# A cosformer-attention and GEGLU kernel: the first two tiles of batch 0 normalised side by side, and the turning of q tile 2 moved

## The chip, the cores and the metric

One core of one Trainium2 chip. The metric is device microseconds of one execution; lower is better. Most executions of a kernel agree within 0.3%, which here is 1 us.

## The reference

```python
def _attn_ref(q, k, v):                      # q, k, v: (8, 8, 576, 64) fp32
    ...
    def phi(x, c, s):
        r = np.maximum(x, 0.0)
        return np.concatenate([r * c, r * s], axis=-1)
    q_p = phi(q, cos_w, sin_w); k_p = phi(k, cos_w, sin_w)
    kv = np.einsum('bhsf,bhsd->bhfd', k_p, v)
    z = np.sum(k_p, axis=2)
    num = np.einsum('bhsf,bhfd->bhsd', q_p, kv)
    den = np.einsum('bhsf,bhf->bhs', q_p, z)[..., None] + 1e-06
    return num / den
# x = attention output as (4608, 512); then
# out = (gelu(x @ w_gate) * (x @ w_val)) @ w_out       with d_ff = 1536
```

The attention has no softmax. Each batch needs one 128x65 product per head ("kv", with the sum z as its 65th column), and then a numerator and a norm for each tile of 128 positions. The feed-forward part is the bulk of the work.

## The kernel before

The instruction streams are written by hand, and each engine runs its stream in program order. Block 0 of the feed-forward part needs x of batch 0, so the attention of batch 0 is a prologue that nothing can hide. The helpers and the prologue that the change touches:

```python
def numer_mm(b, t, bank, g, rows=128):           # numerators of 4 heads of tile t
    for h in range(4 * g, 4 * g + 4):
        nc.tensor.matmul(ps[0:rows, bank + g, ...], lhsT=qT[b % 2][:, t, h, 0:rows], rhs=kv[b % 2][:, h, 0:D + 1], ...)

def norm(xb, bank, g0, g1, rows=128):            # den = z-column + EPS; rec = 1/den; xb = numerator * rec
    ...
def x_by_pe(b, t, xb, bank, eng, c0=0, c1=CT):   # turn x on PE, copy to xT on eng
    ...
def q_by_pe(b, j, bank, eng, h0=0, h1=H):        # turn q tile j on PE; q_evac copies it to SBUF
    ...

# ... (cut)
kv_half(0, 0, 4, None)                           # heads 0 to 3
q_evac(0, 1, 1, "v")
dummies(2)
cast_v(0, 4, 6, "v")
cast_v(0, 6, 8, "s")
kv_evac(0, 0, 4, "v")
kv_half(0, 1, 5, "s")                            # heads 4 to 7
x0, x1 = new_xb(), new_xb()
numer_mm(0, 0, 6, 0)
norm(x0, 6, 0, 1)
dummies(1, 4)
numer_mm(0, 0, 6, 1)
sq(2, 1, "s")
norm(x0, 6, 1, 2)
sq(2, 0, "v")
numer_mm(0, 1, 0, 0)
numer_mm(0, 1, 0, 1)
norm(x1, 0, 0, 2)
x_by_pe(0, 0, x0, 4, "s", 0, 2)
dummies(2, 5)
x_by_pe(0, 0, x0, 4, "s", 2, 4)
q_by_pe(0, 2, 3, None)
# ... (cut: weight load, helpers)
gate(0, 0, 0, 128, 5)
gate(0, 1, 0, 128, 4)
X(1, 2, "s")()                                   # turn x of tile 1
q_evac(0, 2, 3, "v")
sq(3, 0, "v"), sq(3, 1, "s")
value(0, 0, 0, 128, 6)
value(0, 1, 0, 128, 7)
Y(2, 0)()                                        # numerators and norm of tile 2
gate(0, 0, 128, 128, 5)                          # "the second gate pair"
gate(0, 1, 128, 128, 4)
```

"v" is VectorE (DVE), "s" is ScalarE (ACT), PE is TensorE. To turn a tile is to transpose it by matmuls with the identity; the result is then copied from PSUM to SBUF ("evacuated") before the next matmul reads it. A gate and a value are the two products with the weights of a feed-forward unit, gelu(gate) times value is its result. The dummies are matmuls without use that keep PE busy.

## Time and profile before

| | before |
|---|---|
| time, median of 6 runs (range) | 325.81 us (325.72 to 325.93) |
| span of the profiled execution | 324.3 us |
| PE busy | 315.1 us, 97% |
| PE's share of the chain that ended last | 93% |
| kv half 1 starts (K) | 13.48 us |
| second-half x transposes of tile 0 start (X) | 16.04 us |
| second gate pair starts (C) | 18.53 us |

A busy share of 97% means that a saving counts only where PE itself waits. K, X and C are the marks that I use throughout. K follows the landing of v's heads 4 to 7 in this kernel. X starts when tile 0 is normalised. From C on the instructions of all kernels here are the same. In the timelines the columns are start, us, engine, line, operation, out<-in, shape, count, and in brackets the idle time before it and what ended that. PE's timeline of the kernel before, just ahead of C:

```profile
17.69 0.61 PE L229 MATMUL ps<-xT,wv_sb 128*128 128x128 bf16 x8
18.14 0.42 PE L170 MATMUL ps<-kv,qT 128*128 128x65 bf16 x8
18.53 0.61 PE L218 MATMUL ps<-xT,wg_sb 128*128 128x128 bf16 x8
```

Values (L229), numerators of tile 2 (L170) and gates (L218) follow each other.

### The profile page before, as it was taken

The page shows a single profiled execution, that of the slowest core. Times are in us where ns is not written, and L with a number is a line of the kernel's source. Part 1 is how long each engine was busy: PE and PEld are TensorE (multiplying, and loading weights), DVE is VectorE, ACT ScalarE, POOL GpSimd, SP SyncE. Part 2 cuts the span into 40 slices and gives each one's busy share as a digit, 9 for nine tenths or more (in the row PEclk, how much of TensorE's full clock was granted, in tenths as well). Part 3 has the DMA queues.
Part 4 walks back from the last instruction along what each step waited for, and adds up shares of the span by engine and source line. Part 5 has one row for each costly group of instructions (what it writes and reads, how often), then busy time and mean ns, then how long its engine had stood idle before and what let it go on. Part 6 is the DMA issues. An engine that isn't in the chain of part 4 may idle for free.

```text
span 324.3 us, 5829 instructions
## 1 busy us (share of the span) xinstructions
PE 315.1 (97%) x2185; PEld 167.1 (52%) x2218; DVE 168.0 (52%) x380; ACT 151.3 (47%) x271; POOL 21.7 (7%) x43
## 2 busy tenths in 40 slices
PE   7899999999999999999999999999999999999994
PEld 3587866455445544544455445544554444444443
DVE  4885776677564576366636574647454222222210
ACT  5674764853583248325642565237522222323321
POOL 2551000001100010001000100010000100100000
PEclk9999999999999999999999999999999999999999
DMA  7999999999899939991999289936333111000124
GB/s 223 287 204 275 226 307 306 324 200 172 282 222 345 219 51 194 333 236 51 195 324 242 50 153 294 301 68 124 104 73 75 32 32 34 32 32 32 37 63 98
DMA packets 88300, 55.56 MB, mean 171 GB/s; under 512 B 53072, under 2 KB 83536, under 8 KB 88272
## 3 DMA queue, kind: packets, MB, share of 16 engines
q1 hardware_dynamic: 81744, 48.84, 60.8%
q0 software_dynamic: 6096, 5.90, 10.2%
q10 hardware_dynamic: 432, 0.46, 0.4%
q8 instruction: 17, 0.28, 0.3%
q14 instruction: 11, 0.09, 0.1%
HBM read 37.75 MB, written 9.44 MB: 146 GB/s over the span
## 4 chain that ended last, share of the span: by engine, by line
PE 93%; DMA 2%; SPq 1%; DVE 1%; issue 1%; POOL 0%; ACT 0%; POOLq 0%; DVEq 0%
PE ps L218 29%; PE ps L229 29%; PE ps L259 28%; PE ps L170 3%; PE ps L154 3%; DMA vf<-in_v_dram 2%; SPq L80 1%; PE ps L277 1%; PE ps L324 1%; PE ps L343 1%; DVE vx L141 0%; ACT xT L346 0%; DVE qp L135 0%; POOL vf L98 0%; POOL qf L97 0%
## 5 line engine op out<-in xcount | busy, mean ns | idle before, releaser
L234 DVE TENSOR_TENSOR hT<-gel,ps 128x512 bf16<-128x512 f32 (+5 forms) x126 | 76.1, 607 | 89.3 <-PE ps L229 88.4
L218 PE MATMUL ps<-xT,wg_sb 128*128 128x512 bf16 (+5 forms) x492 | 111.8, 348 | 0.7
L229 PE MATMUL ps<-xT,wv_sb 128*128 128x512 bf16 (+5 forms) x496 | 111.8, 348 | 0.4
L223 ACT ACTIVATE gel<-ps 128x512 f32<-128x512 f32 (+5 forms) x126 | 67.4, 536 | 74.2 <-PE ps L218 51.9
L259 PE MATMUL ps<-wo_sb,hT 128*128 128x512 bf16 x408 | 94.3, 379 | 0.6
L218 PEld LDWEIGHTS <-wg_sb 128*128 128x128 bf16 x504 | 47.1, 98 | 44.5
L229 PEld LDWEIGHTS <-wv_sb 128*128 128x128 bf16 x504 | 45.7, 98 | 39.0
L259 PEld LDWEIGHTS <-hT 128*128 128x128 bf16 x420 | 40.8, 98 | 47.7
L288 ACT COPY o_sb<-ps 128x512 f32<-128x512 f32 x35 | 20.5, 586 | 76.2 <-PE ps L259 69.9
L185 DVE TENSOR_TENSOR xb<-ps,rec 128x512 bf16<-128x512 f32 (+2 forms) x41 | 27.8, 678 | 2.8 <-DMA xr<-xb 1.4
L182 DVE TENSOR_SCALAR den<-ps 128x8 f32<-128x8 f32 (+2 forms) x41 | 6.7, 163 | 42.2 <-PE ps L170 42.2
L137 ACT ACTIVATE kp<-kf,sin_c 128x512 bf16<-128x512 f32 (+1 forms) x41 | 25.4, 681 | 0.8 <-DMA kf<-in_k_dram 0.8
L170 PEld LDWEIGHTS <-qT 128*128 128x128 bf16 (+1 forms) x320 | 15.1, 98 | 8.3 <-issue 0.4
L137 ACT ACTIVATE qp<-qf,sin_c 128x512 bf16<-128x512 f32 x28 | 19.3, 713 | 0.1
L135 DVE TENSOR_SCALAR kp<-kf,cos_c 128x512 bf16<-128x512 f32 (+1 forms) x45 | 18.1, 450 | 1.4 <-DMA kf<-in_k_dram 1.4
L135 DVE TENSOR_SCALAR qp<-qf,cos_c 128x512 bf16<-128x512 f32 x40 | 18.2, 495 | 0.0
L209 POOL COPY xT<-xr 128x256 bf16<-128x256 bf16 x7 | 2.8, 402 | 208.7 <-DMA xr<-xb 208.7
L170 PE MATMUL ps<-kv,qT 128*128 128x65 bf16 (+1 forms) x320 | 16.6, 194 | 0.1
L154 PEld LDWEIGHTS <-kp 128*128 128x128 bf16 x320 | 10.9, 97 | 2.6 <-issue 0.7
L127 PE MATMUL ps<-hT 128*128 128x512 bf16 x33 | 10.2, 460 | 1.8 <-DVE par_i L104 1.7
L154 PE MATMUL ps<-vx,kp 128*128 128x65 bf16 x320 | 11.2, 193 | 0.1
L141 ACT CAST vx<-vf 128x1280 bf16<-128x1280 f32 (+1 forms) x9 | 9.7, 1076 | 1.2 <-DMA vf<-in_v_dram 1.2
(54 smaller groups left out, 88.6 us busy)
## 6 DMA issues: line engine op xcount, KB each, us to landing
out_dram<-o_sb SPq DMA_DIRECT2D x38, 128.0 KB, 2.4
kf<-in_k_dram SPq DMA_DIRECT2D x7, 640.0 KB, 7.3
out_dram<-o_sb SPq DMA_DIRECT2D x16, 256.0 KB, 2.9
qf<-in_q_dram SPq DMA_DIRECT2D x6, 640.0 KB, 6.2
vf<-in_v_dram SPq DMA_DIRECT2D x6, 640.0 KB, 8.7
kf<-in_k_dram SPq DMA_DIRECT2D x7, 512.0 KB, 6.2
qf<-in_q_dram SPq DMA_DIRECT2D x6, 512.0 KB, 4.9
vf<-in_v_dram SPq DMA_DIRECT2D x6, 512.0 KB, 7.8
```

The costliest lines, as they stand in the source:

```text
L127: nc.tensor.matmul(ps[:, bank, :], lhsT=junk[:, 0:128], rhs=junk, start=True, stop=True)
L135: nc.vector.tensor_scalar(d, s, col, 0.0, op0=ALU.mult, op1=ALU.max)
L137: nc.scalar.activation(d, s, AF.Relu, scale=col)
L154: nc.tensor.matmul(ps[:, bank, (h % 4) * (D + 1):(h % 4 + 1) * (D + 1)], lhsT=kp[:, j, h, :], rhs=vx[b % 2][:, j, h, 0:D + 1], start=(j == ...
L170: nc.tensor.matmul(ps[0:rows, bank + g, (h % 4) * (D + 1):(h % 4 + 1) * (D + 1)], lhsT=qT[b % 2][:, t, h, 0:rows], rhs=kv[b % 2][:, h, 0:D ...
L185: nc.vector.tensor_tensor(xb[0:rows, g0:g1], nd[:, :, :, 0:D], rec[0:rows, 0:n, :, None].to_broadcast([rows, n, 4, D]), op=ALU.mult,)
L218: nc.tensor.matmul(ps[:, gb, 0:w], lhsT=wg_sb[:, ct, jt * 128:(jt + 1) * 128], rhs=xT[:, ct, p0:p0 + w], start=(ct == 0), stop=(ct == CT - 1),
L223: nc.scalar.activation(gel[:, 0:w], ps[:, gb, 0:w], AF.Gelu)
L229: nc.tensor.matmul(ps[:, vb, 0:w], lhsT=wv_sb[:, ct, jt * 128:(jt + 1) * 128], rhs=xT[:, ct, p0:p0 + w], start=(ct == 0), stop=(ct == CT - 1),
L234: nc.vector.tensor_mul(hT[n % 2][:, jt, 64 + c0:64 + c0 + w], gel[:, 0:w], ps[:, vb, 0:w])
L259: nc.tensor.matmul(ps[:, bank, :], lhsT=hT[n % 2][:, jt, c0:c0 + 128], rhs=wo_sb[:, jt, :], start=(jt == 0), stop=(jt == JT - 1),)
L288: nc.scalar.copy(o_sb, ps[:, bank, :])
```

## The change

Its intent: normalise tiles 0 and 1 together by halves of heads, so that the norms of heads 0 to 3 run while kv's second half is still being made, and tile 1 is ready much sooner. To make room, a k scale goes to ACT and half a q scale to DVE, kv half 0 begins with the heads whose cast is done first and is copied on ACT, and the turning of q tile 2 goes behind the first gates. Along with this the first-half copy of tile 0's x goes to DVE, and some scales and dummies move. The core of the diff (left out are the split of `value` and of `x_by_pe` into two functions each, which changes no instruction by itself, the line that makes `xp`, where tiles 0 and 1 are kept, and the argument `heads` of `kv_half`):

```diff
@@ -187,6 +188,19 @@
             rec[0:rows, 0:n, :, None].to_broadcast([rows, n, 4, D]), op=ALU.mult,
         )
 
+    def norm_pair(bank, g, n):
+
+        nd = ps[:, bank:bank + 2, 0:4 * (D + 1)].rearrange("p t (h e) -> p t h e", e=D + 1)
+        den = rot.tile([128, 2, 4], FP32, name="den")
+        nc.vector.tensor_scalar(den, nd[:, :, :, D], EPS, None, op0=ALU.add)
+        rec = rot.tile([128, 2, 4], FP32, name="rec")
+        nc.vector.reciprocal(rec, den)
+        for t in range(0, 2, n):
+            nc.vector.tensor_tensor(
+                xp[:, t:t + n, g], nd[:, t:t + n, :, 0:D],
+                rec[:, t:t + n, :, None].to_broadcast([128, n, 4, D]), op=ALU.mult,
+            )
+
     def new_xb():
         return rot.tile([128, 2, 4, D], BF16, name="xb", bufs=4)
... (cut)
@@ -356,47 +380,47 @@
     for h0 in (0, 4):
         for j in range(NJ + 1):
             sk(j, 0, "v", h0, h0 + 4)
-            sk(j, 1, "v" if j < 2 else "s", h0, h0 + 4)
+            sk(j, 1, "v" if j < (2 if h0 == 0 else 1) else "s", h0, h0 + 4)
     nc.scalar.copy(wg_sb[0:2, 0, 0:1], qf[0:2, 7, 1, D - 1:D])
     load_w(0, 2)
     load_w(2, 4)
     load_w(4, 8)
-    for j in range(2):
-        sq(j, 0, "v"), sq(j, 1, "s")
-        q_by_pe(0, j, j, None)
-    dummies(3)
+    sq(0, 0, "v"), sq(0, 1, "s", 0, 4), sq(0, 1, "v", 4, 8)
+    q_by_pe(0, 0, 0, None)
+    sq(1, 0, "v"), sq(1, 1, "s")
+    q_by_pe(0, 1, 1, None)
+    dummies(2)
     q_evac(0, 0, 0, "v")
     cast_v(0, 0, 2, "v")
     cast_v(0, 2, 4, "s")
-    kv_half(0, 0, 4, None)
+    kv_half(0, 0, 4, "s", (2, 3, 0, 1))
     q_evac(0, 1, 1, "v")
     dummies(2)
     cast_v(0, 4, 6, "v")
     cast_v(0, 6, 8, "s")
-    kv_evac(0, 0, 4, "v")
+
+    numer_mm(0, 0, 6, 0)
+    numer_mm(0, 1, 7, 0)
     kv_half(0, 1, 5, "s")
-    x0, x1 = new_xb(), new_xb()
-    numer_mm(0, 0, 6, 0)
-    norm(x0, 6, 0, 1)
-    dummies(1, 4)
-    numer_mm(0, 0, 6, 1)
+    norm_pair(6, 0, 2)
+    dummies(1, 3)
+    x_by_pe(0, 0, xp[:, 0], 4, "v", 0, 2)
+    numer_mm(0, 0, -1, 1)
+    numer_mm(0, 1, 0, 1)
+    norm_pair(0, 1, 1)
     sq(2, 1, "s")
-    norm(x0, 6, 1, 2)
-    sq(2, 0, "v")
-    numer_mm(0, 1, 0, 0)
-    numer_mm(0, 1, 0, 1)
-    norm(x1, 0, 0, 2)
-    x_by_pe(0, 0, x0, 4, "s", 0, 2)
-    dummies(2, 5)
-    x_by_pe(0, 0, x0, 4, "s", 2, 4)
-    q_by_pe(0, 2, 3, None)
-
-    nc.gpsimd.tensor_copy(tiny[0:1, 1:2], x0[0:1, 1, 3, D - 1:D])
+    x_by_pe(0, 1, xp[:, 1], 2, "s", 0, 2)
+    dummies(3, 3)
+    x_by_pe(0, 0, xp[:, 0], 4, "s", 2, 4)
+    sq(2, 0, "v"), sq(3, 0, "v")
+    x_by_pe(0, 1, xp[:, 1], 2, "s", 2, 4)
+
+    nc.gpsimd.tensor_copy(tiny[0:1, 1:2], xp[0:1, 0, 1, 3, D - 1:D])
     load_w(8, 12)
 
 
     A, Bw = (0, 256), (256, 320)
-    xs = {1: x1}
+    xs = {}
 
     def X(t, bank, eng):
         return lambda: x_by_pe(0, t, xs[t], bank, eng)
@@ -408,9 +432,8 @@
 
     gate(0, 0, 0, 128, 5)
     gate(0, 1, 0, 128, 4)
-    X(1, 2, "s")()
-    q_evac(0, 2, 3, "v")
-    sq(3, 0, "v"), sq(3, 1, "s")
+    sq(3, 1, "s")
+    q_by_pe(0, 2, 3, "v")
     value(0, 0, 0, 128, 6)
     value(0, 1, 0, 128, 7)
     Y(2, 0)()
```

More of the change, by code (lines that the diff above doesn't have):

```diff
@@ L71 @@
     junk = hT[1][:, 0, 0:512]
+    xp = hT[1][:, 1:3, 0:512].rearrange("p t (g h d) -> p t g h d", g=2, h=4)
     ident = sb.tile([128, 128], BF16, name="ident")
@@ L148, in turn_q, with kv_half @@
         )
-    def kv_half(b, g, bank, eng="s"):
-        for h in range(4 * g, 4 * g + 4):
+    def kv_half(b, g, bank, eng="s", heads=None):
+        for h in heads or range(4 * g, 4 * g + 4):
             for j in range(NJ + 1):
@@ L223, in gate, with value @@
         nc.scalar.activation(gel[:, 0:w], ps[:, gb, 0:w], AF.Gelu)
-    def value(n, jt, c0, w, vb):
+    def value(n, jt, c0, w, vb, now=True):
         p0 = starts[n] + c0
@@ L232, in value, with product @@
             )
+        if now:
+            product(n, jt, c0, w, vb)
+    def product(n, jt, c0, w, vb):
         gel = gels.pop((n, jt, c0))
@@ L336, in x_by_pe @@
     def x_by_pe(b, t, xb, bank, eng, c0=0, c1=CT):
-        p0 = b * S + t * 128
-        cp = nc.vector.tensor_copy if eng == "v" else nc.scalar.copy
         xb2 = xb.rearrange("p g h d -> p (g h d)")
@@ L345, in x_by_pe, with x_evac @@
             )
+        if eng is not None:
+            x_evac(b, t, bank, eng, c0, c1)
+    def x_evac(b, t, bank, eng, c0=0, c1=CT):
+        p0 = b * S + t * 128
+        cp = nc.vector.tensor_copy if eng == "v" else nc.scalar.copy
+        rows = 128 if t < NJ else 64
+        view = ps[:, bank, 0:256].bitcast(BF16).rearrange("p (c t) -> p c t", c=CT)
         cp(xT[:, c0:c1, p0:p0 + rows], view[:, c0:c1, 0:rows])
```

## The prediction

> **What bounds the kernel now.** I read the page first (busy shares, chain), then the chain in order of time over the first 40 us, then the timelines of PE, VectorE (DVE) and ScalarE (ACT) over 9 to 25 us.
>
> ```profile
> PE 315.1 (97%) x2185; PEld 167.1 (52%) x2218; DVE 168.0 (52%) x380; ACT 151.3 (47%) x271; POOL 21.7 (7%) x43
> ...
> PE 93%; DMA 2%; SPq 1%; DVE 1%; issue 1%; POOL 0%; ACT 0%; POOLq 0%; DVEq 0%
> ```
>
> PE is 97% busy and 93% of the chain. The change touches nothing after the first units of block 0, and from 26 us the chain is PE all the way to the output copies at the end. So the change is worth exactly what it shifts PE's stream by, at the moment where that stream has become dense. That moment is in the prologue, shown by the chain in order of time (start us, us, what):
>
> ```profile
> 6.25 6.45 DMA vf<-in_v_dram
> ...
> 12.80 0.64 DVE vx L141
> ...
> 13.48 0.76 PE ps L154 x20
> ...
> 15.89 0.49 DVE qp L135
> ...
> 16.42 0.62 PE ps L324 x8
> 17.04 0.45 PE ps L218 x8
> 17.49 0.37 PE ps L343 x4
> 17.86 0.45 PE ps L229 x8
> 18.30 0.25 PE ps L170 x8
> 18.56 0.58 PE ps L218 x8
> 19.14 0.45 PE ps L229 x8
> ```
>
> The start is bound by the transfer of v's heads 4 to 7, which lands at 12.7. Then follow the cast of those heads, the second kv half, numerators and norms of tiles 0 and 1, and at 16.42 the q transposes of tile 2, which waited for a DVE scale and stand ahead of the first gate matmul. From 17.04 on it is PE. I call the start of the second pair of gates (the line at 18.56; 18.53 in PE's own timeline) the **checkpoint**: from there to 23.4 PE has no gap in either order of work, and the instructions after it are the same in both kernels. What holds the checkpoint in the kernel before is seen on DVE and ACT (columns: start, us, engine, line, operation):
>
> ```profile
> 16.71 0.69 DVE L185 TENSOR_TENSOR xb<-ps,rec 128x512 bf16<-128x512 f32 x1
> 17.32 0.68 DVE L332 COPY qT<-ps 128x1024 bf16<-128x1024 bf16 x1
> 17.92 0.48 DVE L135 TENSOR_SCALAR qp<-qf,cos_c 128x512 bf16<-128x512 f32 x1
> ```
>
> ```profile
> 16.35 0.37 ACT L346 COPY xT<-ps 128x256 bf16<-128x256 bf16 x1 [0.37 <-PE ps L343]
> 17.30 0.50 ACT L223 ACTIVATE gel<-ps 128x128 f32<-128x128 f32 x2 [0.58 <-PE ps L218]
> 17.89 0.59 ACT L346 COPY xT<-ps 128x512 bf16<-128x512 bf16 x1
> ```
>
> Tile 1's x is complete at 17.40, its evacuation ends at 18.48, and the gates that read it start at 18.53. The evacuation of q tile 2 (17.32 to 18.00) is done before its numerators want it at 18.14.
>
> **What the Trainium skill says.** (1) "TensorE: Matmul & The Clock Gate", section "Back-to-back issue gap", gives 134 cycles of 2.4 GHz, 56 ns, for a warm isolated 128-column matmul, and about 81 ns for streams with weight loads. This trace sides with the first: 8 gate matmuls of 128 columns advance the chain by 0.45 us, 56 ns each. (2) "VectorE: DVE Perf Modes", section "The TRN2 errata", gives (N+151)/0.96 ns for an fp32 tensor_tensor, so 691 ns at 512 elements and 424 at 256. The norm multiplications took 0.69 and 0.42 us: pairing two tiles in one instruction saves the fixed part, about 0.15 us, not half. (3) "PSUM — Partial Sum Buffer", section "Engine vs sequencer instructions": the ScalarE and VectorE queues are strict FIFO and matmuls start in program order. So a numerator matmul that waits holds the gates behind it even if their inputs are there. This trace agrees in that no engine's order differs from the program's.
>
> **The change part by part.** Durations are those of the rows before; a handover between engines is 0.04 us (den at 14.40, ends 14.56, next at 14.60). On one engine the next independent instruction starts about 0.08 before the end of the last (TT 15.55+0.42, next at 15.89).
>
> 1. *k scale moved to ACT, q tile 0's second scale split.* DVE is at q 0.26 us sooner, but q lands only at about 9.4 (ACT waited for it until 9.43). ACT runs one more half scale in time it had idle (0.40 us), then a half and a full scale in place of two full ones: sin of tile 1 ends near 10.63 instead of 10.85, q transposes of tiles 0 and 1 start near 10.06 and 10.68 (10.29 and 10.90). DVE copies them at 10.72 and 11.80. All 0.2 sooner, all ahead of the v transfer, so worth nothing by itself.
>
> 2. *kv half 0 in the order 2,3,0,1, evacuated on ACT.* Starts after ACT's cast (ends 11.82) at 11.86 instead of 12.16, ends 12.62, ACT evacuates 12.66 to 13.04 (before: DVE, to 13.76). ACT's last v cast slips from 12.78 to about 12.97 and ends 13.69.
>
> 3. *Numerators of heads 0 to 3 of both tiles before kv half 1.* Eight matmuls at 13.08, done 13.48. kv half 1 still starts at 13.47 when DVE's cast (DMA-bound, unchanged) ends; its last heads wait for ACT's cast until 13.73 and end near 14.24: unchanged. ACT evacuates to 14.66, also unchanged. Gained: the first pair of norms runs in this shadow, den 13.52, reciprocal 13.72, product 13.95 to 14.64, where DVE had 0.65 us idle and one quarter of the work.
>
> 4. *Heads 4 to 7.* x transposes of the first half at 14.68, numerators of both tiles right behind, done about 15.2. DVE evacuates the x half (0.29, from 15.00), then den 15.24, reciprocal 15.44, products 15.67 to 16.09 (tile 0) and 16.01 to 16.43 (tile 1). Before: 15.97 and 17.40. So **tile 0 is 0.1 later, tile 1 is 1.0 earlier**. Second-half transposes at 16.13 and 16.47, ACT's copies 16.45 to 16.82 and 16.79 to 17.16.
>
> 5. *q tile 2's transposes moved behind the first gates.* The first two gate matmuls need only the first half and run before; the third waits for 16.82 and starts at 16.86. Six matmuls by 56 ns end at 17.19. So the gates, begun at 16.88 before, are done 0.14 sooner. But now the rest: q transposes 17.19 to 17.63 (8 by 56 ns), values 17.63 to 18.08, then numerators of tile 2. These need q tile 2 in SBUF: from the start of transposes to the start of their copy took 0.65 us (10.29 to 10.95, and 19.42 to 20.07), so DVE copies from 17.84 to 18.53 and the numerators start at 18.57, **0.5 us after PE is free**. Eight numerators take 0.25: checkpoint 18.82.
>
> Sum for PE after the first gate. Before: 16.88 + gates 0.45 + x transposes 0.22 + values 0.45 + numerators 0.25 + wait for tile 1's copy 0.28 = 18.53. After: 16.86 + rest of gates 0.33 + q transposes 0.45 + values 0.45 + wait for q's copy 0.49 + numerators 0.25 = 18.83. **Net +0.3 us.** Behind the checkpoint all waits (such as the gates at 24.27 on the copy of tile 3) hang on work that PE itself started, so I expect the shift to be kept in full. Weights don't matter: the first gate pair landed at 9.92 + 5.9 = 15.8, the first value pair at 10.80 + 6.3 = 17.1, both before use. The later loads start 0.1 to 0.3 later and are not waited for by PE in the kernel before.
>
> 325.84 + 0.3 gives 326.1.
>
> **Rivals.** (a) *The gain passes through.* If q's copy were in time, the checkpoint would be near 18.34 and the kernel 0.2 us faster, 325.6. For it: tile 1 is ready a microsecond sooner and 0.22 us of transposes leave the dense part. Against it: the copy is 0.68 us of DVE, cannot start before the transposes end, and only 0.45 us of values stand between. (b) *The pairing itself delays.* The first-half transposes stand in front of the second numerators in PE's queue; if the paired product (two banks in one access) ends later than 14.64, the second norms, both tiles and the first gate slip with it. At 0.2 us more this makes 326.3 to 326.4. For it: only 0.02 us of room between 14.64 and kv half 1's evacuation at 14.66. Against: the 512-element product has taken 0.69 in every occurrence of the prologue. (c) *Nothing is seen.* The two changes cancel: 325.8. (d) *The clock falls* from other pauses in the prologue; all stretches up to 300 us were granted 1.00, and the pauses I find (0.3 to 0.4 us) are no longer than those before, so I give it little.
>
> **Range and chances.** (a) to (c) span 325.6 to 326.4; the three runs before spread by 0.12 us. With a little for another execution I take 325.5 to 326.6. A 2% change would be 6.5 us, more than the whole stretch concerned (13.1 to 18.5) has to give: within 2% is nearly certain.
>
> **What would show each step.** First-half product ends near 14.64; tile 0's x near 16.1, tile 1's near 16.4; third gate matmul near 16.86; numerators of tile 2 start near 18.57, released by the copy of q tile 2 on DVE, with about 0.5 us of PE idle before; second gate pair near 18.8, and everything after shifted by the same. The step most likely to be wrong is the last: if the numerators start by 18.1 without a wait, rival (a) holds. If the second den starts later than 15.3, rival (b) holds. A shift at 30 us that differs from that at the checkpoint would mean slack that I missed.

## The result

| | before | changed |
|---|---|---|
| median of 6 runs (range) | 325.81 us (325.72 to 325.93) | 326.18 us (325.67 to 326.45) |
| ratio, 95% interval | | 1.0009 (0.9996 to 1.0022) |
| span of the profiled execution | 324.3 us | 324.3 us |
| K, X, C | 13.48, 16.04, 18.53 | 13.27, 16.08, 18.82 |

Ratios are the mean time of one kernel's fast runs over that of the other's of the same rounds, so not quite the ratio of the medians. The verdict is "same" at 2%. A difference of 0.3 us is 0.1%, so the interval alone can't tell it from none.

The lines of the page after that answer to those shown of before:

```profile
PE 315.3 (97%) x2185; PEld 167.0 (51%) x2218; DVE 168.2 (52%) x378; ACT 151.5 (47%) x273; POOL 21.9 (7%) x43
...
PE 93%; DMA 2%; DVE 1%; issue 1%; SPq 1%; ACT 0%; POOL 0%; POOLq 0%; ACTq 0%; DVEq 0%
```

Hardly anything moved there. The chain in order of time shows the difference (start us, us, what; line numbers are those of the changed kernel: L155 kv, L171 numerators, L199 the paired product, L232 gates, L342 and L350 turning and copying of q, L359 x transposes):

```profile
4.92 5.91 DMA vf<-in_v_dram
...
11.70 0.76 PE ps L155 x20
...
13.82 0.70 DVE hT L199
...
16.83 0.49 PE ps L232 x6
17.32 0.46 PE ps L342 x8
...
17.81 0.70 DVE qT L350
...
18.56 0.43 PE ps L171 x8
18.98 0.45 PE ps L232 x8
```

Two things are new. The chain now leaves PE once more at 17.81, for the copy of q tile 2. And it goes back to v's first heads (kv half 0 at 11.70, the paired product) instead of the last. PE's timeline shows the wait as such:

```profile
17.16 0.61 PE L342 MATMUL ps<-ident,qp 128*128 128x128 bf16 x8
17.61 0.61 PE L243 MATMUL ps<-xT,wv_sb 128*128 128x128 bf16 x8
18.56 0.43 PE L171 MATMUL ps<-kv,qT 128*128 128x65 bf16 x8 [0.34 <-DVE qT L350]
18.82 0.61 PE L232 MATMUL ps<-xT,wg_sb 128*128 128x128 bf16 x8
```

The eight values take PE 0.45 us from 17.61, so PE could start the numerators at 18.06; they start at 18.56. The bracket counts 0.34 us, because it takes the modelled end of the last value matmul instead of the time when PE could have begun the next.

The shift of 0.3 us is kept to the very end. The last group of matmuls and the last copy, before:

```profile
316.85 2.78 PE L277 MATMUL ps<-wo_sb,hT 128*128 128x256 bf16 x24
319.97 0.29 DVE L282 COPY o_sb<-ps 128x128 f32<-128x128 f32 x1 [0.97 <-ACT o_sb L281]
```

and after:

```profile
317.15 2.78 PE L295 MATMUL ps<-wo_sb,hT 128*128 128x256 bf16 x24
320.27 0.29 DVE L300 COPY o_sb<-ps 128x128 f32<-128x128 f32 x1 [0.97 <-ACT o_sb L299]
```

From C to the last group it is 298.32 us before and 298.33 after. The two spans are still equal, because the time from the last copy's end to the end of the span was 4.0 us in the profiled execution of before (324.3 - 320.26) and 3.7 in that of the changed kernel (324.3 - 320.56). The end of the last output transfer moves by as much as the effect. That execution of before took 326.12 us, more than all six timed ones.

### The profile page after: what moved, and what is told of

It is laid out like the page before. It is cut to its first block, busy times and chain, and to the rows that moved or that the text cites. A ratio compares the mean times of both kernels' runs of the same rounds, so it can differ in the third digit from the quotient of the medians.

```text
span 324.3 us, 5828 instructions
## 1 busy us (share of the span) xinstructions
PE 315.3 (97%) x2185; PEld 167.0 (51%) x2218; DVE 168.2 (52%) x378; ACT 151.5 (47%) x273; POOL 21.9 (7%) x43
## 4 chain that ended last, share of the span: by engine, by line
PE 93%; DMA 2%; DVE 1%; issue 1%; SPq 1%; ACT 0%; POOL 0%; POOLq 0%; ACTq 0%; DVEq 0%
PE ps L232 29%; PE ps L243 28%; PE ps L277 28%; PE ps L171 3%; PE ps L155 3%; DMA vf<-in_v_dram 2%; PE ps L295 1%; PE ps L359 1%; SPq L81 1%; PE ps L342 1%; DVE hT L199 0%; ACT vx L142 0%; DVE qT L350 0%; ACT xT L370 0%; POOL vf L99 0%
## 5 line engine op out<-in xcount | busy, mean ns | idle before, releaser
L232 PE MATMUL ps<-xT,wg_sb 128*128 128x512 bf16 (+5 forms) x492 | 112.0, 348 | 0.7
L232 PEld LDWEIGHTS <-wg_sb 128*128 128x128 bf16 x504 | 47.0, 98 | 44.7
L183 DVE TENSOR_SCALAR den<-ps 128x8 f32<-128x8 f32 (+1 forms) x38 | 6.3, 165 | 41.7 <-PE ps L171 41.5
L186 DVE TENSOR_TENSOR xb<-ps,rec 128x512 bf16<-128x512 f32 (+1 forms) x38 | 26.3, 691 | 2.8 <-DMA xr<-xb 1.5
L171 PEld LDWEIGHTS <-qT 128*128 128x128 bf16 (+1 forms) x320 | 15.1, 98 | 8.9 <-DVE qT L350 0.5
L138 ACT ACTIVATE qp<-qf,sin_c 128x512 bf16<-128x512 f32 (+1 forms) x28 | 19.1, 706 | 0.1
L171 PE MATMUL ps<-kv,qT 128*128 128x65 bf16 (+1 forms) x320 | 16.6, 194 | 0.4 <-DVE qT L350 0.3
L155 PEld LDWEIGHTS <-kp 128*128 128x128 bf16 x320 | 10.9, 97 | 2.2 <-issue 0.4
L155 PE MATMUL ps<-vx,kp 128*128 128x65 bf16 x320 | 11.2, 193 | 0.1
```

Of the source, the lines that this page charges most:

```text
L138: nc.scalar.activation(d, s, AF.Relu, scale=col)
L155: nc.tensor.matmul(ps[:, bank, (h % 4) * (D + 1):(h % 4 + 1) * (D + 1)], lhsT=kp[:, j, h, :], rhs=vx[b % 2][:, j, h, 0:D + 1], start=(j == ...
L171: nc.tensor.matmul(ps[0:rows, bank + g, (h % 4) * (D + 1):(h % 4 + 1) * (D + 1)], lhsT=qT[b % 2][:, t, h, 0:rows], rhs=kv[b % 2][:, h, 0:D ...
L186: nc.vector.tensor_tensor(xb[0:rows, g0:g1], nd[:, :, :, 0:D], rec[0:rows, 0:n, :, None].to_broadcast([rows, n, 4, D]), op=ALU.mult,)
L232: nc.tensor.matmul(ps[:, gb, 0:w], lhsT=wg_sb[:, ct, jt * 128:(jt + 1) * 128], rhs=xT[:, ct, p0:p0 + w], start=(ct == 0), stop=(ct == CT - 1),
```

## The experiments

Twelve runs of ten kernels were made, in four series, each next to the kernel before on the same chip. All gave correct results. The marks:

| run | K | X | C | X - K | C - X | median us | ratio to before (95%) |
|---|---|---|---|---|---|---|---|
| before | 13.48 | 16.04 | 18.53 | 2.56 | 2.49 | 325.81 | |
| before again | 13.19 | 15.75 | 18.32 | 2.56 | 2.57 | 325.93, one run | |
| changed | 13.27 | 16.08 | 18.82 | 2.81 | 2.74 | 326.18 | 1.0009 (0.9996 to 1.0022) |
| changed again | 13.05 | 15.81 | 18.55 | 2.76 | 2.74 | 326.06 | 1.0009 (0.9997 to 1.0022) |
| e1, q turned ahead of the gates | 13.43 | 16.32 | 18.72 | 2.89 | 2.40 | 325.89 | 1.0000 (0.9987 to 1.0014) |
| e2, before with q behind the gates | 12.81 | 15.38 | 18.70 | 2.57 | 3.32 | 326.85 | 1.0027 (1.0012 to 1.0042) |
| e3, q in two halves | 13.62 | 16.51 | 18.96 | 2.89 | 2.45 | 325.85 | 1.0006 (0.9993 to 1.0019) |
| e4, q in the pause | 13.12 | 15.85 | 17.63 | 2.73 | 1.78 | 325.48 | 0.9993 (0.9981 to 1.0006) |
| e4 again | 13.34 | 16.04 | 17.81 | 2.70 | 1.77 | 325.19 | 0.9983 (0.9970 to 0.9995) |
| e5, before with parts 1 and 2 | 13.05 | 15.65 | 18.14 | 2.60 | 2.49 | 325.77 | 0.9997 (0.9982 to 1.0012) |
| e6, changed without part 2 | 13.76 | 16.64 | 19.38 | 2.88 | 2.74 | 326.77 | 1.0025 (1.0008 to 1.0042) |
| e7, e4 and e8 together | 12.95 | 15.63 | 17.40 | 2.68 | 1.77 | 326.12 | 1.0011 (0.9997 to 1.0024) |
| e8, numerators first | no ordinary trace | | | | | 326.86 | 1.0033 (1.0020 to 1.0047) |
| e8 again | 12.86 | 15.46 | 18.20 | 2.60 | 2.74 | 326.67 | 1.0028 (1.0012 to 1.0045) |

K scatters by several tenths between executions even where everything before it is the same. C by itself is therefore no clean measure; X - K and C - X are better. C - X holds the first gates and q tile 2 (part 5 of the prediction) and, in the kernel before, also the turning of tile 1 and the waits for it; X - K holds the norms (parts 3 and 4).

In the kernels with paired numerators, one more mark is needed: kv half 1 stands behind these numerators in PE's queue. Call their start N, as here in the changed kernel:

```profile
12.93 0.41 PE L171 MATMUL ps<-kv,qT 128*128 128x65 bf16 x8
13.27 0.77 PE L155 MATMUL ps<-vx,kp 128*128 128x65 bf16 x20
13.87 0.38 PE L128 MATMUL ps<-hT 128*128 128x512 bf16 x1
14.57 0.29 PE L359 MATMUL ps<-ident,hT 128*128 128x128 bf16 x2 [0.32 <-DVE hT L199]
14.69 0.42 PE L171 MATMUL ps<-kv,qT 128*128 128x65 bf16 x8
...
16.08 0.61 PE L359 MATMUL ps<-ident,hT 128*128 128x128 bf16 x4 [0.21 <-DVE hT L199]
```

N is 12.93 and 12.66 in the two traces of the changed kernel, 13.18 in e1, 13.36 in e3 and 13.51 in e6. X - N is 3.15, 3.15, 3.14, 3.15 and 3.13, while X - K runs from 2.76 to 2.89. So X of these kernels follows N, and with it v's first heads, and not K. In e1, e3 and e6 K itself is 0.25 or 0.26 after N, the time of the eight numerators, and so held by them.

**The two kernels again.**

> The changed kernel unaltered, timed again beside the others. Main theory (the numerators of tile 2 wait for the copy of q tile 2, everything after is shifted by the same): second gate pair again at 18.8 (within 0.2, as the input transfers land some tenths earlier or later), last matmul group about 0.3 later than in the kernel before, median 0.3 us above the kernel before. Rival (the 0.37 us between the medians is only scatter of the transfers at the two ends): the sign of the difference changes or it falls under 0.1 us.

> The kernel before, unaltered, for a second trace of it: how much the landing of the input transfers and the end of the last output transfer move from execution to execution. Expected from the trace of the changed kernel: k, q and v land up to 0.4 us earlier or later; the second gate pair moves with v's heads 4 to 7 by 0.2 us at most; the time from the end of the last copy to the end of the span moves by 0.3 us.

The changed kernel's C was 18.55 and its median 0.20 above before (326.06 against 325.86), with the same ratio, 1.0009. The sign held; the size is at the lower end, and neither interval excludes 1. C was 0.25 under the 18.8 expected, a little more than the 0.2 allowed. The last matmul group started at 316.88: 0.23 later than in the second trace of before (316.65), but only 0.03 later than in the first. In the second trace of before, K and X came 0.29 earlier, but C only 0.21: the value matmuls waited 0.2 us for their weights (the view of the weight loads' waits):

```profile
PEld L229 <- DMA wv_sb<-in_moe_w_val_dram: 0.2, 1, 0.2
```

The time from the last copy to the end was 4.0 us again and did not move by the 0.3 expected. So v's landing and the weights' landing are nearly equal limits, which the prediction had denied for the weights.

**e1: only the placement of q tile 2 undone.**

```diff
     x_by_pe(0, 1, xp[:, 1], 2, "s", 2, 4)
+    q_by_pe(0, 2, 3, None)
 ...
     sq(3, 1, "s")
-    q_by_pe(0, 2, 3, "v")
+    q_evac(0, 2, 3, "v")
```

> Only the placement of q tile 2 undone: its transposes again ahead of the first gate, its copy again right after them, the rest of the change kept. Main theory: transposes 16.79 to 17.24 (they wait for the scale on DVE), gates to 17.69, values to 18.14, copy on DVE 17.44 to 18.13, numerators without a long wait near 18.17, second gate pair near 18.4: 0.4 earlier than in the changed kernel, 0.1 earlier than before; time 325.7 where before is 325.8. Rival (the pairing costs the 0.3 us): second gate pair stays at 18.8 or later and the time stays at 326.1 to 326.2.

C - X fell from 2.74 to 2.40, near the 0.4 expected, and the wait is gone:

```profile
17.95 0.61 PE L243 MATMUL ps<-xT,wv_sb 128*128 128x128 bf16 x8
18.45 0.43 PE L171 MATMUL ps<-kv,qT 128*128 128x65 bf16 x8
18.72 0.61 PE L232 MATMUL ps<-xT,wg_sb 128*128 128x128 bf16 x8
```

The numerators now follow at 18.45, 0.05 after PE is free. The time came out level with before (ratio 1.0000), though 325.7 was expected. In the profiled execution 0.27 of the gain was lost again behind C (298.60 us from C to the last group), in part between 60 and 75 us, where numerators of a later batch waited for a DMA that turns q. C itself was only 0.1 earlier than in the changed kernel, because kv half 0 was held up by v's first heads in this execution (the timeline shows a pause of 0.30 in the middle of kv half 0, and N is 0.25 later than in the changed kernel). The placement, not the pairing, causes this part of the loss.

**e2: the kernel before with only the placement changed.**

```diff
     x_by_pe(0, 0, x0, 4, "s", 2, 4)
-    q_by_pe(0, 2, 3, None)
 ...
     X(1, 2, "s")()
-    q_evac(0, 2, 3, "v")
+    q_by_pe(0, 2, 3, "v")
```

> The kernel before with only the placement of q tile 2 changed: its transposes behind the first gates and behind tile 1's x transposes, its copy right after. Main theory: gates 16.76 to 17.2, x transposes 17.44 to 17.66, q transposes to 18.1, values to 18.55, copy on DVE 18.3 to 19.0, numerators near 19.03 after a wait of 0.5, second gate pair near 19.3: 0.7 to 0.8 later than before; time 326.5. Rival (the placement is harmless, the pairing costs): second gate pair within 0.2 of 18.5.

C - X rose from 2.49 to 3.32, by 0.83, and the median by 1.0 us (mean by 0.9, ratio 1.0027). The same wait stands in the trace:

```profile
18.43 0.43 PE L170 MATMUL ps<-kv,qT 128*128 128x65 bf16 x8 [0.34 <-DVE qT L332]
```

By itself the move is harmful: it costs 0.8 us in the kernel before. (C alone, at 18.70, would have fitted the rival's "within 0.2 of 18.5": K was 0.67 earlier in this execution.) In the changed kernel the earlier tile 1 pays most of that back: from the third gate matmul to C it is 1.99 us there and 2.59 in e2, where the gates end at 16.44 and the transposes of tile 1 then take PE until 17.02.

**e3: q tile 2 in two halves.**

```diff
-    q_by_pe(0, 2, 3, "v")
+    q_by_pe(0, 2, 3, "v", 0, 4)
+    q_by_pe(0, 2, 2, "v", 4, 8)
```

> The changed kernel with q tile 2 turned in two halves of four heads, each into its own bank and copied by itself, both on DVE; placement as in the change. Main theory: the first copy starts near 17.57 and ends near 17.97, the second ends near 18.3, numerators of heads 0 to 3 start right after the values near 18.06 and those of heads 4 to 7 near 18.35; second gate pair near 18.5, 0.3 earlier than in the changed kernel; time about that of before (325.8). Rival: no effect on the second gate pair (18.8), time 326.1 to 326.2.

C - X is 2.45, so 0.29 less than in the changed kernel, as expected. (C itself was 18.96 instead of 18.5, as N was 0.43 later than in the changed kernel.) The first half's copy starts when four transposes are done, and both copies are done at 18.77:

```profile
18.01 0.76 DVE L350 COPY qT<-ps 128x512 bf16<-128x512 bf16 x2 [0.30 <-PE ps L342]
```

Here the placement is that of the change and only the copy is quicker to be of use. That the wait shrinks shows that the copy is what PE waits for. The median was level with before, the mean ratio 1.0006, too wide to tell from either.

**e4: q tile 2 in the pause.**

```diff
     norm_pair(6, 0, 2)
+    sq(2, 0, "v")
 ...
-    dummies(3, 3)
+    q_by_pe(0, 2, 3, None)
+    dummies(1)
     x_by_pe(0, 0, xp[:, 0], 4, "s", 2, 4)
-    sq(2, 0, "v"), sq(3, 0, "v")
+    q_evac(0, 2, 3, "v")
+    sq(3, 0, "v")
 ...
     sq(3, 1, "s")
-    q_by_pe(0, 2, 3, "v")
```

> The changed kernel with q tile 2 moved into the pause of PE between the numerators of heads 4 to 7 and the second-half transposes (where three dummy matmuls stood): its scale on DVE right behind the paired product, its copy behind the products of heads 4 to 7. Main theory: the transposes run near 15.3 to 15.8 and cost PE nothing; the copy is done by 17.0; gates end near 17.2, values near 17.6, numerators follow without a wait, second gate pair near 17.9: 0.9 earlier than in the changed kernel, 0.6 earlier than before; time 325.2, which would beat both. Rival (something else holds the second gate pair, such as the gelus, the value weights or the pairing): second gate pair at 18.3 or later, gain under 0.3 us.

> The version with q tile 2 in the pause, timed again, as its five rounds left the interval across 1. If its gain is real: median 0.3 to 0.6 us under before again, second gate pair again 6.2 after the start of kv half 0, and again a wait of about 0.2 us on the weights of the third gate. If the first measurement was scatter: within 0.1 of before.

The transposes took the place of dummy matmuls, and C - X fell to 1.78, 0.96 less than in the changed kernel:

```profile
15.10 0.62 PE L342 MATMUL ps<-ident,qp 128*128 128x128 bf16 x8 [0.17 <-DVE den L195]
...
17.38 0.42 PE L171 MATMUL ps<-kv,qT 128*128 128x65 bf16 x8
17.63 0.61 PE L232 MATMUL ps<-xT,wg_sb 128*128 128x128 bf16 x8
```

The gain in time is smaller than 0.96. The medians were 325.48 against 325.86 before, and on another chip 325.19 against 325.73, with an interval below 1 only the second time (0.9970 to 0.9995). So it is faster than the kernel before, by 0.4 and 0.5 us, and by the medians of the first series 0.6 faster than the changed kernel (326.06). Against the kernel before, C - K is 0.54 to 0.58 less (4.51 and 4.47 instead of 5.05). Two tenths go to a new wait after C, in both traces, for the weights of the third gate (columns: engine and line, what it waited for, us in total, times, longest):

```profile
PEld L232 <- DMA wg_sb<-in_moe_w_gate_dram: 0.2, 1, 0.2
```

**e5: the kernel before with parts 1 and 2 alone** (the k scale and half q scale moved, kv half 0 in the order 2,3,0,1 and copied on ACT).

```diff
-            sk(j, 1, "v" if j < 2 else "s", h0, h0 + 4)
+            sk(j, 1, "v" if j < (2 if h0 == 0 else 1) else "s", h0, h0 + 4)
 ...
-    kv_half(0, 0, 4, None)
+    kv_half(0, 0, 4, "s", (2, 3, 0, 1))
 ...
-    kv_evac(0, 0, 4, "v")
```

> The kernel before with only the shifted k scale, the split q scale, and kv half 0 in the order 2,3,0,1 with its copy on ACT. Step 1 and 2 of the prediction say: q transposes 0.2 earlier, kv half 0 0.3 earlier, but kv half 1 waits for the transfer of v as before, so numerators of tile 0, tile 1's x and the second gate pair stay within 0.1 of 18.5 once the landing of v is allowed for; time within 0.1 of before. Rival: some of it reaches PE, second gate pair 0.2 or more earlier or later relative to the start of kv half 1 than in the kernel before (5.05 us).

C - K is 5.09 against 5.05 in the kernel before, and the ratio 0.9997. By themselves these parts are worth nothing that can be seen.

**e6: the changed kernel without part 2.**

```diff
-    kv_half(0, 0, 4, "s", (2, 3, 0, 1))
+    kv_half(0, 0, 4, None)
 ...
     cast_v(0, 6, 8, "s")
+    kv_evac(0, 0, 4, "v")
```

> The changed kernel with kv half 0 again in order and copied on DVE behind the cast of v's heads 4 and 5. Main theory: part 2 is what lets the paired numerators run ahead of kv half 1; without it they start near 13.6 to 13.8, hold kv half 1 behind them, the paired product ends near 15.2, the third gate matmul slips to about 17.5 and the second gate pair to about 19.4: 0.6 later than in the changed kernel, time 326.8. Rival (part 2 is worth nothing here either): second gate pair within 0.2 of 18.8.

It came out as expected. The paired numerators wait for DVE's copy of kv half 0 and hold kv half 1 behind them:

```profile
13.51 0.41 PE L171 MATMUL ps<-kv,qT 128*128 128x65 bf16 x8 [0.62 <-DVE kv L167]
13.76 0.76 PE L155 MATMUL ps<-vx,kp 128*128 128x65 bf16 x20
```

DVE's last cast of v, which usually releases kv half 1, ended at 13.12 in this trace, so K came 0.6 late, and the median was 326.77. Part 2 is worth nothing alone and 0.6 us as a condition of part 3.

**e8 and e7: the numerators of heads 4 to 7 ahead of the x transposes.**

```diff
-    x_by_pe(0, 0, xp[:, 0], 4, "v", 0, 2)
     numer_mm(0, 0, -1, 1)
     numer_mm(0, 1, 0, 1)
     norm_pair(0, 1, 1)
     sq(2, 1, "s")
+    x_by_pe(0, 0, xp[:, 0], 4, "s", 0, 2)
```

> The changed kernel with the numerators of heads 4 to 7 ahead of tile 0's first-half x transposes in PE's queue, and that half's copy on ACT instead of DVE. It tests the small remainder of rival (b): in the changed kernel these numerators start 0.25 us after kv's second half is in SBUF, because the transposes in front of them wait for the paired product. If so: numerators within 0.05 us of the end of that copy, tile 0's second-half transposes 0.25 earlier against the start of kv half 0 (4.13 instead of 4.38 after it), second gate pair 0.25 earlier against it (6.87 instead of 7.11), the wait of tile 2's numerators on the q copy unchanged at 0.5; time 0.2 to 0.25 us under the changed kernel, about that of before. If the paired product's place is harmless: second gate pair still 7.1 after the start of kv half 0.

> q tile 2 in the pause, and the numerators of heads 4 to 7 ahead of the transposes, together. If work on PE's path is all there is: second gate pair 0.25 earlier than with the pause alone (5.97 instead of 6.22 after the start of kv half 0), and the time 0.25 under it. If the weights of the third and fourth gate are the next limit, as the 0.2 us wait on them in the trace with the pause alone suggests: the second gate pair is earlier, but the wait on the weights before the third gate grows by the same 0.25 to about 0.4, and the time is that of the pause alone within 0.1.

> The same kernel as the numerators-first run, whose one profiled execution fell in a state with every matmul at about half rate (677 us in all) and whose four other executions took 326.83 to 326.94, 1.1 us above before and 0.9 above what was expected. A trace of an ordinary execution is wanted. If the reordering itself costs: second gate pair 0.5 or more later than the expected 6.87 after the start of kv half 0, with a wait in front of it to be named. If it is the state of PE in that series: second gate pair at 6.87 and the time at 325.8 to 326.0 this time.

The first series of e8 had one execution of 678.84 us, the profiled one, in which every matmul took about twice as long; it is left out of all comparisons. The other four took 326.83 to 326.94. The second series gave 326.34 to 326.88 and an ordinary trace:

```profile
14.09 0.41 PE L171 MATMUL ps<-kv,qT 128*128 128x65 bf16 x8 [0.25 <-ACT kv L167]
```

The numerators start 0.05 after kv's second half is copied (ACT from 13.66 to 14.04), and X - K fell to 2.60, by 0.2, to about what it is in the kernel before. Not all of this is the edit's: K is 0.47 after N here, and 0.34 and 0.39 in the changed kernel, and X - N fell only from 3.15 to 3.07. Against kv half 0 the gain at C was small (18.20 - 11.16 = 7.04 instead of 7.11, where 6.87 was expected), because v's second half landed later against its first in this execution. And the time rose, against both forecasts. The loss lies behind C: a DVE product starts 1.1 us after its value matmuls (20.63) where 0.71 is usual, the norm of tile 3 behind it comes late, and PE waits for it. On DVE and PE:

```profile
21.74 0.42 DVE L252 TENSOR_TENSOR hT<-gel,ps 128x256 bf16<-128x256 f32 x1 [0.53 <-ACT qp L138]
```

```profile
23.26 0.40 PE L359 MATMUL ps<-ident,xb 128*128 128x128 bf16 x4 [0.22 <-DVE xb L186]
```

In e7 the product is as late (1.12 us after its values at 20.40). C came 6.16 us after the start of kv half 0 (11.24), no earlier than in e4 (6.22 and 6.15), where 5.97 was expected: the numerators' place gained nothing there. The wait on the weights of the third gate is longer than in e4:

```profile
19.13 0.61 PE L232 MATMUL ps<-xT,wg_sb 128*128 128x256 bf16 x4 [0.23 <-DMA wg_sb<-in_moe_w_gate_dram]
```

That fits the weights as the next limit: C is early (17.40), because v landed early, yet the third gate starts at 19.13, as in e4 (19.14; 19.35 in its second trace). But e7 was 0.9 us slower than e4 in the same series (326.12 against 325.19), which the weights do not explain; both forecasts for e7 failed. Why that product starts 0.4 late in these two kernels stays open. The semaphore values that it waits for in the built programs correspond to the same instructions as in the changed kernel, and the releasers that the trace infers differ between the two. From C to the last group e8 lost 0.38 us (298.71 instead of 298.33), which is less than the time shows.

## Why the prediction was right

**The time and the checkpoint.** 326.1 was predicted, 326.18 and 326.06 measured; the checkpoint 18.82, measured 18.82 and 18.55. The hit at 18.82 is closer than the working deserves. The prediction has N at 13.08 and C 5.74 us later; measured are N at 12.93 and C 5.89 later, in the second trace 12.66 and 5.89. What steps 4 and 5 took longer, 0.10 from N to X and 0.05 from X to C, was made up by v's first heads landing earlier than in the trace that the working started from. That is luck.

**Step 5 (q tile 2 behind the gates) held in each term.** The third gate matmul was predicted at 16.86 and measured at 16.83, the copy from 17.84 and measured from 17.81, the numerators at 18.57 and measured at 18.56, after PE had nothing to do for 0.5 us. C - X was predicted to rise from 2.49 to 2.69 and rose to 2.74. It is not this step alone: the turning of tile 1 leaves it at the same time. e1 and e3 take the wait away by two different routes and get 0.34 and 0.29 back; e2 creates it alone, for 0.83. That is shown, not argued. One term of the sum for before is misread, which doesn't change the sum: "wait for tile 1's copy 0.28" is two waits. The gates are done at 17.33, the transposes of tile 1 start at 17.46, after its product (17.40), and only 0.14 is the wait for its copy ahead of 18.53.

**Step 4 (heads 4 to 7) was mis-sized against v's landing.** "Tile 0 is 0.1 later, tile 1 is 1.0 earlier" came out as 0.07 (16.04 against 15.97) and 1.04 (16.36 against 17.40). But in that trace kv half 1 had started 0.2 earlier. Measured from K, tile 0's transposes are 0.2 to 0.25 later (2.76 and 2.81 instead of 2.56). The term that was too small is the one for "numerators of both tiles right behind": the transposes ahead of them in PE's queue wait for the paired product, which ended at 14.51, and the numerators start at 14.69, though kv's second half was ready at 14.45. e8 takes the hold away and X - K returns to 2.60, in part by the landing of that execution. The prediction's own marks (13.47 and 16.13) give 2.66, so it allowed 0.10 for this hold and the traces show 0.20 and 0.25. So rival (b) is true in a small size. Its "only 0.02 us of room" was the right warning; the steady 0.69 us of the product, held against it, was measured again, but the product starts 0.55 us after K (13.82 - 13.27) where the working has 0.48.

Together the two steps cost 0.4 to 0.5 us from K to C (5.05 and 5.13 in the traces of before, 5.55 and 5.50 in those of the changed kernel), where 0.3 was predicted. The medians differ by 0.37 and 0.20. The rest is K itself, which fell 0.21 and 0.14 earlier in the traces of the changed kernel than in those of before. Where the numerators do not hold it, K moves from 12.81 to 13.48 over the runs without order, so I take this for scatter, and it isn't settled. As X of the changed kernel follows N, the distance between the landings of v's two halves is part of it.

**Steps 1 to 3 held.** Steps 1 and 2 are worth nothing alone (e5), and step 2 is what step 3 needs (e6, 0.6 us). The first paired norm runs in the shadow of kv half 1, its product from 13.82 to 14.51 (predicted 13.95 to 14.64).

**The other rivals.** Rival (a) needed q's copy in time, and the trace shows that it was not. e4 shows what the intent could have gained: with q tile 2 turned in PE's pause, C - X is 0.96 us less than in the changed kernel. Rival (c), that nothing is seen, the times alone can't exclude; the marks, 0.4 to 0.5 us more from K to C in both traces, speak against it. Of rival (d) nothing was seen: the granted clock was at least 0.996 in every fast run of both kernels.

**"Weights don't matter" was too strong.** It is true of the changed kernel. In the second trace of before, in e4 and in e7 PE waited 0.2 to 0.4 us for them: they land only just in time.

**"The shift to be kept in full"** held: 298.32 and 298.33 us from C to the last matmuls in the two traces of before, 298.33 in both of the changed kernel. It is no law of this kernel: e1 took 298.60 and e5 298.56, though both keep everything behind C as it is.

## What to carry to other kernels

Moving work behind the first users of PE is free only if its whole chain (transpose, copy, next matmul) fits under what stands between; here 0.65 us from the first transpose to the copy plus 0.7 us of copy met 0.9 us of work on PE (the transposes themselves and the values), and the difference became a wait. Look for a pause that is already filled with dummies and put the chain's PE part there, early enough that its copy ends before it is wanted. When effects are as small as the scatter of transfers, measure between marks that a transfer does not move, and check with a second trace of the kernel before how far it does. When a change puts work in front of a mark, as the numerators in front of kv half 1, see whether the mark still follows what it followed.

## What the Trainium skill lacked or had wrong

- "TensorE: Matmul & The Clock Gate", section "Back-to-back issue gap": the sustained figures for streams with a weight load ahead of each matmul (about 81 ns at 128 columns, 131 at 512) do not hold here. Eight gate matmuls of 128 columns with eight weight loads take 0.45 us, 56 ns each, and 12 output matmuls of 512 columns take 2.59 us, 216 ns each: the page's isolated figures.
- The same page, section "The HAM clock gate", has a throttle that sustained activity releases after some 3.4 us, with the caveat that it has been seen stuck for over 50 us. One execution of e8 kept matmuls at about half rate to the end, with PE busy 99% of 676.6 us; four gates of 512 columns took 2.05 us where 1.03 is usual. Its recorded granted clock was 1.000, so it isn't shown that this throttle was the cause, and what put it there is not known.
- "VectorE: DVE Perf Modes", section "The TRN2 errata": the formula (N+151)/0.96 ns for an fp32 tensor_tensor also fits products that read PSUM and write bf16 (0.69 us at 512 elements, 0.42 at 256). The page does not say that it covers PSUM; the PSUM row of its table for VectorE, 120 + FD cycles, would give less (estimates from that row: 0.66 and 0.39 us).
- No page that I read for this case says how much the landing of transfers moves between executions. Here kv half 1, which follows the landing of v, started anywhere from 12.81 to 13.48 us where the numerators did not hold it, and the last output transfer ended 3.7 to 4.0 us after the last copy.
